# Dependences by bank in a wide PSUM buffer, and branch bits made one product later, in an attention and mixture-of-experts kernel

## Chip, cores and metric

One NeuronCore of a Trainium2 chip runs the whole program. The metric is the device time of one execution in microseconds (us), as the median of several. The engines are TensorE (PE, matrix products; PEld is its weight load, PEq and PEldq its sequencer), VectorE (DVE), ScalarE (ACT), GpSimd (POOL) and SyncE (SP, which issues most DMAs). Each engine works through its own instructions in order; semaphores hold one engine back for another.

## What is computed

An attention with queries averaged in pairs makes 2304 rows of 512, and these go through a mixture of 8 experts, of which each row uses its best two:

```python
q_pool = q.reshape(B, H, S // factor, factor, D).mean(axis=3)
scores = scale * np.matmul(q_pool, k.transpose(0, 1, 3, 2))
...
attn_out = np.matmul(attn, v)                    # 4 x 8 x 576 x 64 -> 2304 x 512
...
noisy_logits = logits + noise_scale * noise
top2 = np.argpartition(-noisy_logits, 2, axis=1)[:, :2]
...
for e in range(E):
    for k in range(2):
        mask = top2[:, k] == e
        h = np.maximum(x[mask] @ w1[e], 0.0)
        out[mask] += top2_w[mask, k, None] * (h @ w2[e])
```

Inputs and output are float32. Products of the experts are made of three fp16 products (high by high, high by low, low by high), so x, h and the weights each exist as a high and a low half.

## The kernel before

The attention and the routing are issued in an order that a planner (`Plan`) sets ahead of time from costs and due times. As soon as rows of a batch are routed, POOL scatters them, sorted by expert, to a buffer xg in DRAM, and DMA transposes bring them back as columns. The experts then run in `Moe`:

- `early` is still planned. It works on the first 256 rows (`EARLY`) of experts 0, 1 and 2 while the last batch is being routed. For each of the 8 slices f of the hidden layer, `one` calls `mm1`: 12 matmuls of 128x256 (L1067), four chunks of the inner dimension by three fp16 products. Then `act` makes hh, the high half of the relu, on ACT (L1131), and `low` makes hl, the rest, on DVE (L1135). For experts 0 and 1 the second layer follows (`mm2`, L1102, and `out_y`, L1107).
- `run` is in the order in which it is written. For expert 0 it takes rows 256 to 608 (`CUT`), so each main product is 12 matmuls of 128x352 out of xTg, and `flush` makes hh (ACT L1094) and hl (DVE L1095). After the eighth product `tail` holds rows 608 to 640 behind a branch: PE compares bit e of the register `s.more` and skips the block if the expert has no more rows than that. The bits come from four small DVE operations on the row counts (full, L1174 to L1178), and `values_load` (L1179) brings them into PE's register. Both stand before the first main product.

PSUM holds four single banks (psm) and two wide buffers of two banks each, `s.B.wides` (pss_63 and pss_64 in the program). A main product takes a wide buffer. An early product takes one half, that is one bank, from the pool "half": half 0 and half 1 of pss_63, half 0 and half 1 of pss_64, and again. The framework keeps track of dependences by the whole buffer: an instruction on one half that writes, or reads what was written, is ordered behind the last accesses of the other engines to either half.

The other names are: mk, a mask of the routing, which DVE makes (L870) for a small matmul (L873); mg, the gate factors that DVE makes in `meta` (L1050); wh and wl, the high and low halves of weights, split by ACT (L1016) and DVE (L1018); sp, a single element that POOL copies out of xTg (L1170) so that POOL waits for that transpose.

Of the kernel before, what the change touches and what calls it, by code (L numbers as in the profile page):

```python
# [9 lines left out]
F32 = mybir.dt.float32  # L10
I32 = mybir.dt.int32
U32 = mybir.dt.uint32
U16 = mybir.dt.uint16
AF = mybir.ActivationFunctionType
ALU = mybir.AluOpType
AX = mybir.AxisListType
# [3 lines left out]
P = 128  # L20
# [8 lines left out]
E = 8  # L29
# [3 lines left out]
CUT = 608  # L33
# [3 lines left out]
EARLY = 256  # L37
# [183 lines left out]
class Attn:  # L221
# [137 lines left out]
    def max_fin(s, i, c, g):  # L359
        V = s.nc.vector  # L360
        mx, qn2 = s.maxes(i), s.G.buf["qn2", i]
        m = s.rest(i, g)[:, SG:SG + c.stop - c.start]
        V.reduce_max(m, mx[:, c], axis=AX.X)
        V.tensor_scalar(qn2[:, c, 64], m, -1.0 / MC, None, op0=ALU.mult)
        V.scalar_tensor_tensor(qn2[:, c, 65], m, -1.0 / MC, qn2[:, c, 64], op0=ALU.mult, op1=ALU.subtract)

# [292 lines left out]
class Route:  # L659
# [111 lines left out]
    def steps(s, j, gs, tag, gap, L=None):  # L771
        nc = s.nc
        V = nc.vector
        C = 3 * len(gs)
# [26 lines left out]
        yield  # L801
        V.tensor_scalar(a, a, 87.0, None, op0=ALU.min)
        yield
# [134 lines left out]
class Moe:  # L938
# [115 lines left out]
    def mm1(s, e, f, a=0, b=CUT, ps=None):  # L1054
        nc = s.nc
        hi, lo = s.W[e, "1"]
        xT = s.X[e, a]
        hh, hl = s.H[e]
        if ps is None:
            ps = s.B.wide()  # L1060
        m = 1 if b - a <= 512 else 2
        N = (b - a) // m
        n = 0
        for dc in range(4):
            for w, x in ((hi, 0), (hi, 1), (lo, 0)):
                for i in range(m):
                    nc.tensor.matmul(ps[:, i, 0:N], w[:, dc, f * P:(f + 1) * P],  # L1067
                                     xT[:, 2 * dc + x, i * N:(i + 1) * N], start=(n == 0), stop=(n == 11))
                n += 1
        v = lambda t: t[:, f, a:b].rearrange("p (a n) -> p a n", a=m)  # L1070
        s.late.append((v(hh), v(hl), ps[:, 0:m, 0:N]))

    def tail(s, e, a):
        nc = s.nc
        n = CAP - CUT
        hi, lo = s.W[e, "1"]
        xT = s.X[e, a]
        hh, hl = s.H[e]
        ps = s.B.bank()[:, 0:8 * n].rearrange("p (f n) -> p f n", n=n)
        with s.tc.If((s.more & (1 << e)) > 0, preferred_fallthrough_block=False):  # L1080
            for f in range(8):
                k = 0
                for dc in range(4):
                    for w, x in ((hi, 0), (hi, 1), (lo, 0)):
                        nc.tensor.matmul(ps[:, f], w[:, dc, f * P:(f + 1) * P], xT[:, 2 * dc + x, CUT - a:CAP - a],
                                         start=(k == 0), stop=(k == 11))
                        k += 1
        s.late.append((hh[:, :, CUT:CAP], hl[:, :, CUT:CAP], ps))
        s.flush()
# [27 lines left out]
    def early(s, A):  # L1117
        G = A.G
        op = G.op
        nc = s.nc  # L1120
        A.M = s
        s.W[0, "1"] = s.F0.w
        for e in range(E):
            s.H[e] = s.H[e % 2] if e > 1 else tuple(s.h.tile([P, 8, CAP], F16, name=f"h{x}") for x in "hl")
        fl, ld, done = {}, {}, {}
        G.pool("half", [t[:, a] for t in s.B.wides for a in range(2)])
        last = None

        def act(e, f):
            hh, _, ps = fl[e, f]  # L1130
            nc.scalar.activation(hh, ps, AF.Relu)  # L1131

        def low(e, f):
            hh, hl, ps = fl[e, f]
            nc.vector.scalar_tensor_tensor(hl, ps, 0.0, hh, op0=ALU.max, op1=ALU.subtract)  # L1135

        def one(e, f):
            s.mm1(e, f, 0, EARLY, G.buf["m", e, f][:, None, :])
            fl[e, f] = s.late.pop()

        los = []
        A.xe[2] = op("SP", 1.4, LATE + 21, lambda: s.xload(2, 0, EARLY), lat=4.0)
        for x in range(16):
            e, nm, c = s.loads[x]
            key = LATE + (2, 13.512, 24.696, 36)[x // 4] + (2, 2.5, 2.5, 2.5)[x // 4] * c
            hi = op("ACT", 1.06, key, lambda e=e, nm=nm, c=c: s.split(e, nm, c, 0), deps=[ld[x]] if x in ld else ())
            los.append(op("DVE", 1.14, key, lambda e=e, nm=nm, c=c: s.split(e, nm, c, 1, False), deps=[hi]))
            for y in (4, 5, 6) if x == 0 else (x + 6,) if x < 4 else (x + 4,) if 5 < x < 12 else ():
                last = ld[y] = op("SP", 0.6, key, s.load, deps=los[x:x + 1] if y > 5 else (), lat=5.0, after=last)
            done.setdefault((e, nm), []).append(los[-1])  # L1150
        done[0, "1"] = [A.f0]
        for e in range(NFIRST):
            k0 = LATE + (-4.156, 23, 41.252)[e]
            mm, lows = None, []
            if e < NEARLY:
                mt = op("DVE", 0.8, k0 + 16, lambda e=e: s.meta(e, 0, EARLY), deps=[A.xe[e]])
            for f in range(8):
                mm = op("PE", 1.28, k0 + 1.3 * f, lambda e=e, f=f: one(e, f), deps=(done[e, "1"][f // 2:f // 2 + 1] if e else done[e, "1"]) + [A.xe[e]],
                        take=[("half", ("m", e, f))], after=mm)
                hi = op("ACT", 0.3, k0 + 1.3 * f + 1, lambda e=e, f=f: act(e, f), deps=[mm])  # L1160
                lows.append(op("DVE", 0.33, k0 + 1.3 * f + 1.5, lambda e=e, f=f: low(e, f), deps=[hi], give=[("m", e, f)]))
            for b in range(2 if e < NEARLY else 0):
                for q in range(4):
                    mm = op("PE", 1.28, k0 + 12 + 5 * b + 1.3 * q, lambda e=e, b=b, q=q: s.mm2(e, b, (2 * q, 2 * q + 1), G.buf["y", e, b]),
                            deps=lows[2 * q:2 * q + 2] + done[e, "2"][q:q + 1] if b == 0 else (), take=[("bank", ("y", e, b))] if q == 0 else (), after=mm)
                op("ACT", 0.55, k0 + 17 + 5 * b, lambda e=e, b=b: s.out_y(e, b, G.buf["y", e, b]), deps=[mm, mt], give=[("y", e, b)])
        G.run()

    def run(s):
        s.nc.gpsimd.tensor_copy(s.B.sp, s.X[0, EARLY][0:1, 7, CAP - EARLY - 1:CAP - EARLY])  # L1170
        s.put()
        V = s.nc.vector
        full = s.sm.tile([P, E + 1], F32, name="full", bufs=1)
        V.tensor_scalar(full[:, 0:E], s.R.n0, float(CUT), None, op0=ALU.is_gt)  # L1174
        V.tensor_mul(full[:, 0:E], full[:, 0:E], s.two)
        V.reduce_sum(full[:, E:E + 1], full[:, 0:E], axis=AX.X)
        mi = s.sm.tile([P, 1], I32, name="full_i", bufs=1)
        V.tensor_copy(mi, full[:, E:E + 1])  # L1178
        s.more = s.nc.values_load(mi[0:1, 0:1], engines=[mybir.EngineType.PE], min_val=0, max_val=(1 << E) - 1,  # L1179
                                  skip_runtime_bounds_check_because="it is only compared")  # L1180
        s.B.nw = 1
        for _ in range(4):
            s.load()
        for e in range(E + 1):
            if e == E:
                s.nc.gpsimd.drain()
            if e < E:
                if e == 2:
                    s.meta(e, 0, EARLY)
                s.meta(e, EARLY if e < NFIRST else 0, CAP)  # L1190
                for f in range(8):
                    s.mm1(e, f, EARLY if e < NFIRST else 0)
                    s.flush()
                    if 2 <= e < E - 1:
                        s.split(e + 1, "1", f // 2, f % 2)
                s.tail(e, EARLY if e < NFIRST else 0)
                if 1 <= e < E - 1:
                    s.xload(e + 1, EARLY if e + 1 < NFIRST else 0, CAP)
            if e:
                for k, b in enumerate(range(2 if e <= NEARLY else 0, NB)):  # L1200
                    if 2 <= e < E:
                        for c in ((k,), (k,), (2, 3))[k] if e == 2 else ((k,) if k < 4 else ()):
                            s.split(e, "2", c)
                    ps = s.B.bank()
                    s.mm2(e - 1, b, range(8), ps)
                    s.out_y(e - 1, b, ps)
# [142 lines left out]
```

## Time and profile before

| | |
|---|---|
| median of 3 runs | 849.32 us (849.32, 845.66, 850.34) |
| profiled execution | 846.78 us, its span 845.0 us |
| granted clock of PE over the span | 0.994 of full speed |
| busy share of PE, DVE, ACT, POOL | 93%, 60%, 53%, 49% |
| 412 to 476 us (early products) | PE busy 56.01 of 64 us |
| 476 to 508 us (expert 0, main products, tail) | PE busy 30.65 of 32 us |
| 508 to 836 us (the other experts) | PE busy 324.83 of 328 us |

A shown start and duration are those of one row of the trace. In square brackets at a row's end stands how long the engine was idle before it, and which instruction's semaphore released it. The end of a matmul is modelled: a row of x12 back to back lasts less than 12 single ones, since matmuls are pipelined.

### The profile page before, as it was taken

What the parts mean: (1) busy time and instruction counts of PE and PEld (TensorE: products, weight loads), DVE (VectorE), ACT (ScalarE), POOL (GpSimd) and SP (SyncE); (2) the same over time, 40 slices, a digit from 0 to 9 for tenths busy, and PEclk for the clock granted to TensorE, in tenths of its full rate; (3) what the DMA queues carried; (4) which work ended last, traced back from release to release, by engine and by line L of the source; (5) the groups of instructions that cost most, each with busy time, mean ns of one, the idle gap of its engine ahead of it and who ended that gap; (6) DMA issues with size and microseconds to landing.
All of it is one profiled execution on the core that took longest, in us unless ns stands there. A gap on an engine that the chain in (4) does not pass through costs nothing. (4 is left out here: it accounts for less than half of the span.)

```text
span 845.0 us, 21305 instructions
## 1 busy us (share of the span) xinstructions
PE 789.9 (93%) x8704; PEld 530.2 (63%) x8704; DVE 508.8 (60%) x1212; ACT 447.3 (53%) x702; POOL 417.2 (49%) x414
## 2 busy tenths in 40 slices
PE   4899899999999999999998899999999999999996
PEld 1666667777677776677855564565564755647442
DVE  5888898979898999999886231543152242422200
ACT  4778778888787777676644222433232332321310
POOL 4689887999789768777336302010202012020122
PEclk9999999999999999999999999999999999999999
DMA  8999988859998994889858902656628364381134
GB/s 202 205 220 214 223 198 204 202 164 211 208 212 187 180 231 103 197 180 264 204 168 284 253 13 31 180 153 140 161 76 225 76 180 95 105 209 13 26 41 61
DMA packets 214652, 137.32 MB, mean 163 GB/s; under 512 B 148240, under 2 KB 185616, under 8 KB 214544
## 3 DMA queue, kind: packets, MB, share of 16 engines
q1 hardware_dynamic: 205904, 115.74, 57.3%
q0 software_dynamic: 8640, 20.08, 11.9%
q8 instruction: 75, 1.23, 0.6%
q14 instruction: 33, 0.27, 0.1%
HBM read 62.14 MB, written 35.44 MB: 115 GB/s over the span
## 5 line engine op out<-in xcount | busy, mean ns | idle before, releaser
L394 POOL TENSOR_TENSOR pl<-pf 128x384 f16<-128x384 f32 x296 | 279.9, 977 | 54.8 <-ACT pf L386 42.1
L100 POOL DMA_INDIRECT out_dram<-y,mti x40 | 62.2, 1556 | 309.3 <-ACT y L1107 288.9
L386 ACT ACTIVATE pf<-pss 128x768 f32<-128x768 f32 x216 | 173.7, 815 | 54.4 <-PE pss L379 43.6
L414 PEld LDWEIGHTS <-pf 128*128 128x128 bf16 x2880 | 154.7, 98 | 47.1 <-issue 20.1
L414 PE MATMUL psm<-vv,pf 128*128 128x65 f16 (+1 forms) x2880 | 165.4, 194 | 5.9 <-DVE mx L338 3.0
L414 PE MATMUL psm<-vv,pl 128*128 128x65 f16 (+1 forms) x1440 | 157.1, 193 | 3.0 <-DVE pl L391 2.1
L378 PE MATMUL pss<-qt,kt 128*128 128x384 f16 (+1 forms) x576 | 147.8, 286 | 3.0 <-ACT pf L386 2.8
L379 PE MATMUL pss<-qt,kt 66*128 66x384 f16 (+1 forms) x576 | 148.3, 287 | 1.2 <-DMA qt<-qn 1.2
L1095 DVE SCALAR_TENSOR_TENSOR hl<-pss,hh 128x608 f16<-128x608 f32 (+1 forms) x64 | 44.3, 692 | 157.4 <-ACT hh L1094 157.0
L414 PEld LDWEIGHTS <-pl 128*128 128x128 f16 x1440 | 126.5, 99 | 5.3 <-issue 2.7
L1102 PE MATMUL psm<-wh,hh 128*128 128x512 f16 x320 | 121.3, 379 | 3.5 <-PEq L1080 3.5
L1102 PE MATMUL psm<-wh,hl 128*128 128x512 f16 x320 | 121.3, 379 | 0.0
L1102 PE MATMUL psm<-wl,hh 128*128 128x512 f16 x320 | 121.3, 379 | 0.0
L1102 PEld LDWEIGHTS <-hh 128*128 128x128 f16 x640 | 62.0, 98 | 78.4 <-issue 5.0
L338 DVE CUSTOM_DVE_ANT_0 rd<-psm,rd 128x512 f32<-128x512 f32 x144 | 97.6, 683 | 18.5 <-ACT rd L334 17.8
L1107 ACT ACTIVATE y<-psm,mg 128x512 f32<-128x512 f32 x40 | 27.5, 686 | 144.9 <-PE psm L1102 73.2
L1094 ACT ACTIVATE hh<-pss 128x608 f16<-128x608 f32 (+1 forms) x64 | 38.2, 597 | 114.1 <-PE pss L1067 114.1
L334 ACT ACTIVATE rd<-psm 128x512 f32<-128x512 f32 x144 | 85.8, 598 | 14.5 <-PE psm L318 12.5
L318 PE MATMUL psm<-kt,qt 128*128 128x128 f16 (+3 forms) x317 | 75.0, 308 | 8.8 <-DVE mx L338 4.1
L391 DVE TENSOR_TENSOR pl<-pf 128x768 f16<-128x768 f32 x68 | 74.5, 1115 | 2.3 <-ACT pf L386 2.3
L379 PEld LDWEIGHTS <-kt 66*128 66x128 f16 x576 | 56.1, 97 | 18.9 <-issue 4.7
L378 PEld LDWEIGHTS <-kt 128*128 128x128 f16 x576 | 56.2, 98 | 17.2 <-issue 4.0
(227 smaller groups left out, 1184.6 us busy)
## 6 DMA issues: line engine op xcount, KB each, us to landing
xg<-zt SPq DMA_DIRECT2D x40, 260.0 KB
kr<-in_k_dram SPq DMA_DIRECT2D x32, 288.0 KB
vr<-in_v_dram SPq DMA_DIRECT2D x16, 576.0 KB
kr<-in_moe_w_dram SPq DMA_DIRECT2D x16, 512.0 KB
qr<-in_moe_w_dram SPq DMA_DIRECT2D x16, 512.0 KB
kn<-in_moe_w_dram SPq DMA_DIRECT2D x16, 512.0 KB
qr<-in_q_dram SPq DMA_DIRECT2D x31, 256.0 KB
vr<-in_moe_w_dram SPq DMA_DIRECT2D x14, 512.0 KB
```

The lines of the kernel that those rows point to most:

```text
L100: i = nc.gpsimd.indirect_dma_start(out=out, out_offset=bass.IndirectOffsetOnAxis(ap=idx, axis=0), in_=src, in_offset=None, **kw)
L318: s.nc.tensor.matmul(ps[r, o:o + m.shape[1] * P], s.G.buf["qt", i][:, c, r], m, start=True, stop=True)
L334: s.nc.scalar.activation(s.G.buf["rd", i, c], s.G.buf["D", i, c], AF.Relu)
L338: s.nc.vector.tensor_tensor_reduce(out=rd, in0=s.G.buf["S", i, c], in1=rd, scale=1.0, scalar=-3.0e38, op0=ALU.add, op1=ALU.max, accum_out= ...
L378: mm(ps[:, a, o:o + w], kt[:, hh * NK + kc, :], qf[:, q0:q0 + w], start=True, stop=False)
L379: mm(ps[:, a, o:o + w], kt2[0:66, hh * NK + kc, :], qf2[0:66, q0:q0 + w], start=False, stop=True)
L386: s.nc.scalar.activation(s.parts(u)[0], s.G.buf["ps", u][:, :, 0:SG], AF.Exp, scale=0.125 / (IN_SCALE * IN_SCALE))
L391: s.nc.vector.tensor_sub(pl, pf, ph)
L394: s.nc.gpsimd.tensor_sub(pl[:, a], pf[:, a], ph[:, a])
L414: mm(o[:, 0:x], src[:, t % 2, ci * P:ci * P + P], vv[:, hh * NK + kc, a:a + x], start=st, stop=last and src is pl, skip_group_check=True)
L1095: s.nc.vector.scalar_tensor_tensor(hl, ps, 0.0, hh, op0=ALU.max, op1=ALU.subtract)
L1102: s.nc.tensor.matmul(ps, h[:, f, b * P:(b + 1) * P], w[:, f, :], start=(f == 0 and k == 0), stop=(f == 7 and k == 2))
```

## The change

Two things. First, `early` notes for each half which instructions touch it, and `apart` declares to the framework that an instruction on one half doesn't depend on an instruction of another engine on the other half of the same buffer ("distinct banks"). `mm1` returns its matmuls for this. Second, the four DVE operations become `counts`, which is called after the flush of the first main product, and the load of the register moves into `tail` of expert 0, ahead of its branch.

```diff
@@ mm1
+        made = []
...
-                    nc.tensor.matmul(ps[:, i, 0:N], w[:, dc, f * P:(f + 1) * P],
-                                     xT[:, 2 * dc + x, i * N:(i + 1) * N], start=(n == 0), stop=(n == 11))
+                    made.append(nc.tensor.matmul(ps[:, i, 0:N], w[:, dc, f * P:(f + 1) * P],
+                                                 xT[:, 2 * dc + x, i * N:(i + 1) * N], start=(n == 0), stop=(n == 11)))
...
+        return made
+
+    def counts(s):
+        V = s.nc.vector
+        full = s.sm.tile([P, E + 1], F32, name="full", bufs=1)
+        V.tensor_scalar(full[:, 0:E], s.R.n0, float(CUT), None, op0=ALU.is_gt)
+        V.tensor_mul(full[:, 0:E], full[:, 0:E], s.two)
+        V.reduce_sum(full[:, E:E + 1], full[:, 0:E], axis=AX.X)
+        s.full = s.sm.tile([P, 1], I32, name="full_i", bufs=1)
+        V.tensor_copy(s.full, full[:, E:E + 1])
@@ tail
         ps = s.B.bank()[:, 0:8 * n].rearrange("p (f n) -> p f n", n=n)
+        if e == 0:
+            s.more = nc.values_load(s.full[0:1, 0:1], engines=[mybir.EngineType.PE], min_val=0, max_val=(1 << E) - 1,
+                                    skip_runtime_bounds_check_because="it is only compared")
         with s.tc.If((s.more & (1 << e)) > 0, preferred_fallthrough_block=False):
@@ early
-        G.pool("half", [t[:, a] for t in s.B.wides for a in range(2)])
+        halves = [t[:, a] for t in s.B.wides for a in range(2)]
+        G.pool("half", halves)
+        used = [[] for _ in halves]
...
+        def apart(e, f, eng, made):
+            k = next(k for k, t in enumerate(halves) if t is G.buf["m", e, f])
+            for i in made:
+                for x, o in used[k ^ 1]:
+                    if x != eng:
+                        s.tc.declare_no_dep(i.ins, o.ins, reason="distinct banks")
+                used[k].append((eng, i))
...
-            nc.scalar.activation(hh, ps, AF.Relu)
+            apart(e, f, "ACT", [nc.scalar.activation(hh, ps, AF.Relu)])
...
-            nc.vector.scalar_tensor_tensor(hl, ps, 0.0, hh, op0=ALU.max, op1=ALU.subtract)
+            apart(e, f, "DVE", [nc.vector.scalar_tensor_tensor(hl, ps, 0.0, hh, op0=ALU.max, op1=ALU.subtract)])
...
-            s.mm1(e, f, 0, EARLY, G.buf["m", e, f][:, None, :])
+            apart(e, f, "PE", s.mm1(e, f, 0, EARLY, G.buf["m", e, f][:, None, :]))
@@ run
-        V = s.nc.vector
-        full = s.sm.tile([P, E + 1], F32, name="full", bufs=1)
...
-        s.more = s.nc.values_load(mi[0:1, 0:1], engines=[mybir.EngineType.PE], min_val=0, max_val=(1 << E) - 1,
-                                  skip_runtime_bounds_check_because="it is only compared")
...
                     s.flush()
+                    if e == f == 0:
+                        s.counts()
```

In the order of instructions, POOL and SP keep theirs. On ACT the rows keep their places and some conditions change. Here is ACT at the first products of expert 1, before the change (the line numbers 1107 and 1131 become 1121 and 1155 after it):

```order
L1107 ACTIVATE y<-psm_68,mg 128x512 [waits PE_49]
L1131 ACTIVATE hh<-pss_63 128x256 [waits PE_49]
L1131 ACTIVATE hh<-pss_63 128x256 [waits DVE_49]
L1131 ACTIVATE hh<-pss_64 128x256 [waits PE_49]
L1131 ACTIVATE hh<-pss_64 128x256 [waits DVE_49]
L1131 ACTIVATE hh<-pss_63 128x256 [waits PE_49]
L1016 ACTIVATE wh_8545<-qr 128x1024 [waits DMAHW5_49]
L1131 ACTIVATE hh<-pss_63 128x256 [waits DVE_49]
```

And ACT at the same place in the changed kernel:

```order
L1121 ACTIVATE y<-psm_68,mg 128x512 [waits PE_49]
L1155 ACTIVATE hh<-pss_63 128x256 [waits PE_49] x2
L1155 ACTIVATE hh<-pss_64 128x256 [waits PE_49] x2
L1155 ACTIVATE hh<-pss_63 128x256 [waits DVE_49,PE_49]
L1016 ACTIVATE wh_8545<-qr 128x1024 [waits DMAHW5_49]
L1155 ACTIVATE hh<-pss_63 128x256 [waits DVE_49,PE_49]
L1016 ACTIVATE wh_8545<-kn 128x1024 [waits DMAHW6_49]
```

The second relu of each pair waited for DVE; now it waits for PE (x2 stands for two rows that read alike).

DVE between the last early products and the first main ones, before:

```order
L1135 SCALAR_TENSOR_TENSOR hl<-pss_64,hh 128x256 [waits Activation_49] x2
L1174 TENSOR_SCALAR full<-n_8739 128x8
L1175 TENSOR_TENSOR full<-full,two 128x8 [waits DVE_49,Pool_49]
L1176 TENSOR_REDUCE full<-full 128x1 [waits DVE_49]
L1178 CAST full_i<-full 128x1 [waits DVE_49]
L1038 TENSOR_SCALAR mq<-mt 128x6 [waits DMAHW4_49]
```

and after (L1109 is what L1095 was, L1078 to L1082 what L1174 to L1178 were):

```order
L1050 TENSOR_SCALAR mg<-mg 128x3 [waits DVE_49]
L1109 SCALAR_TENSOR_TENSOR hl<-pss_63,hh 128x352 [waits Activation_49]
L1078 TENSOR_SCALAR full<-n_8739 128x8
L1079 TENSOR_TENSOR full<-full,two 128x8 [waits DVE_49,Pool_49]
L1080 TENSOR_REDUCE full<-full 128x1 [waits DVE_49]
L1082 CAST full_i<-full 128x1 [waits DVE_49]
L1109 SCALAR_TENSOR_TENSOR hl<-pss_64,hh 128x352 [waits Activation_49]
```

The four operations that make the bits went behind the gate factors (`meta`, ending in mg) and the subtraction of the first main product.

PE at the end of expert 0's main products in the changed kernel; before the change the TENSOR_LOAD stood, with the same list of semaphores, ahead of the first product that reads xTg:

```order
L1068 LDWEIGHTS fl
L1068 MATMUL pss_64<-xTg,fl 128x352
L1092 TENSOR_LOAD full_i [waits DMASW6_49,DMASW7_49,DMASW5_49,DMAHW0_49,DMASW4_49,DMAHW1_49,DMASW3_49,DMAHW2_49,DMASW2_49,DMAHW3_49,DMASW1_49,DMAHW4_49,DMASW0_49,DMAHW5_49,DVE_49,DMAHW6_49,PE_49,DMAHW7_49,Activation_49,Pool_49]
L1094 REGISTER_ALU
L1094 COMPARE_AND_BRANCH
L1094 UNCONDITIONAL_BRANCH [waits PE_49]
L1099 LDWEIGHTS fh
```

The load now stands behind the eighth main product and right ahead of the comparison that needs it.

## Rows read from the trace of the kernel before

**Rows 1.** The page: busy us and share of the span, instructions.

```profile
PE 789.9 (93%) x8704; PEld 530.2 (63%) x8704; DVE 508.8 (60%) x1212; ACT 447.3 (53%) x702; POOL 417.2 (49%) x414
```

**Rows 2.** Stretches: start:end, length, busy us (instructions) of PE, PEld, DVE, ACT, POOL; PEclk, DMA share, GB/s.

```profile
412.00:476.00 64.00, 56.01 (x437) 40.33 (x437) 43.05 (x169) 28.53 (x52) 25.03 (x31) 1.00 0.78 237
476.00:508.00 32.00, 30.65 (x192) 19.22 (x191) 9.19 (x28) 7.54 (x17) 3.12 (x2) 0.95 0.40 89
508.00:836.00 328.00, 324.83 (x1916) 186.96 (x1917) 95.51 (x158) 98.51 (x135) 54.37 (x35) 1.00 0.49 113
475.00:480.00 5.00, 3.56 (x15) 1.95 (x15) 1.27 (x12) 0.46 (x1) 0.00 (x0) 0.73 1.02 328
```

**Rows 3.** PE's waits from 412 to 508 us: total us, times, longest us.

```profile
PE pss L1067 <- DVE hl L1135: 3.9, 3, 1.9
PE pss L1067 <- DVE mg L1050: 3.4, 1, 3.4
PE psm L873 <- DVE mk L870: 1.1, 2, 0.8
PE pss L1067 <- PEq L1080: 0.6, 1, 0.6
```

**Rows 4.** PE in order of time: start us, us, instruction, [idle before <-releaser].

```profile
422.39 0.27 PE L1067 MATMUL pss<-xe,fl 128*128 128x256 f16 x1
423.02 0.38 PE L1067 MATMUL pss<-xe,fh 128*128 128x256 f16 x2 [0.36 <-DVE hl L1135]
...
444.72 0.38 PE L1067 MATMUL pss<-xe,wh 128*128 128x256 f16 x2 [1.59 <-DVE hl L1135]
...
461.15 1.47 PE L1067 MATMUL pss<-w1x 128*128 128x256 f16 x12 [1.95 <-DVE hl L1135]
...
476.44 0.46 PE L1067 MATMUL pss<-xTg,fh 128*128 128x352 f16 x2 [3.38 <-DVE mg L1050]
476.74 0.31 PE L1067 MATMUL pss<-xTg,fl 128*128 128x352 f16 x1
...
481.70 0.46 PE L1067 MATMUL pss<-xTg,fh 128*128 128x352 f16 x2
```

**Rows 5.** ACT in order of time, the first two relus of expert 1.

```profile
441.36 0.38 ACT L1131 ACTIVATE hh<-pss 128x256 f16<-128x256 f32 x1 [2.11 <-PE psm L875]
442.24 0.38 ACT L1131 ACTIVATE hh<-pss 128x256 f16<-128x256 f32 x1 [0.49 <-DVE hl L1135]
```

**Rows 6.** DVE in order of time.

```profile
426.26 0.42 DVE L1135 SCALAR_TENSOR_TENSOR hl<-pss,hh 128x256 f16<-128x256 f32 x1 [1.29 <-ACT hh L1131]
...
441.78 0.43 DVE L1135 SCALAR_TENSOR_TENSOR hl<-pss,hh 128x256 f16<-128x256 f32 x1 [0.44 <-ACT hh L1131]
...
474.80 0.16 DVE L1174 TENSOR_SCALAR full<-n 128x8 f32<-128x8 f32 x1
...
475.46 0.15 DVE L1178 CAST full_i<-full 128x1 int32<-128x1 f32 x1
...
479.90 0.53 DVE L1095 SCALAR_TENSOR_TENSOR hl<-pss,hh 128x352 f16<-128x352 f32 x1 [3.60 <-ACT hh L1094]
```

**Rows 7.** PE's sequencer by line: ns min/median/max, first to last start us.

```profile
L1179 PEldq EVENT_SEMAPHORE  x10: 51/51/3951, 471.0 to 475.8; - x10
L1179 PEldq TENSOR_LOAD <-full_i x1: 491/491/491, 475.9 to 475.9; - x1
...
L1080 PEldq ALU_OP  x8: 36/36/42, 490.2 to 782.2; - x8
L1080 PEldq EVENT_SEMAPHORE  x8: 51/51/51, 492.6 to 784.7; - x8
```

**Rows 8.** POOL in order of time: the twelve scatters' first and last, the copy sp.

```profile
443.99 1.19 POOL L100 DMA_INDIRECT xg<-xr,rta  x1 [3.14 <-ACT hh L1131]
...
459.89 1.72 POOL L100 DMA_INDIRECT xg<-xr,rta  x1 [0.30 <-issue]
...
468.34 0.18 POOL L1170 CAST sp<-xTg 1x1 f32<-1x1 f16 x1 [6.73 <-DMA xTg<-xg]
```

More of the change, by code (lines that the diff above doesn't have):

```diff
@@ L1171, in run @@
         s.put()
-        V = s.nc.vector
-        full = s.sm.tile([P, E + 1], F32, name="full", bufs=1)
[L1174 to L1178, printed above, removed]
-        s.more = s.nc.values_load(mi[0:1, 0:1], engines=[mybir.EngineType.PE], min_val=0, max_val=(1 << E) - 1,
-                                  skip_runtime_bounds_check_because="it is only compared")
         s.B.nw = 1
```

## Prediction, made before the changed kernel was run

> **What bounds the kernel now.** I read the page first, then busy time by stretch, then the waits of TensorE (PE) in the stretch that the diff touches, then that stretch in order of time. PE is busy 93% of the span [rows 1]. From 508 us on it has hardly a hole: 324.83 of 328 us at a granted clock of 1.00 [rows 2]. So whatever comes earlier there comes out at the end, one for one, as long as nothing else becomes late. From 412 to 476 us, where the early products run, PE is busy 56.01 of 64 us [rows 2]. The waits name what it waits for: 3.9 us in three waits for the DVE subtraction L1135, 1.1 us in two waits for the route's mask (mk, L870), 3.4 us in one wait put down to DVE mg [rows 3]. That last one is really the load of the branch bits: the ten semaphore waits of L1179 run from 471.0 to 475.8, one of them 3.951 us long, and the load, at 475.9 for 0.491 us, ends at 476.39, where the first main product starts at 476.44 [rows 4, 7]. The long one waits for the CAST full_i at 475.46 on DVE [rows 6], which stands behind the last early subtractions.
>
> **A stall costs more than its idle figure.** Twelve 128x256 matmuls in a row take 1.47 us and one is shown as 0.27, so starts lie (1.47 − 0.27)/11 = 0.11 apart [rows 4]. The shown idle begins at the modelled end, 0.16 after the next could have started. Each stall costs its figure and 0.16.
>
> **Part 1, the halves.** Before, ACT's relu of half 0 waits for PE's product into half 1, and its relu of half 1 waits for DVE's subtraction in half 0: the row at 442.24 was released by hl, 0.88 us after the relu before it began [rows 5]. PE's next product into half 0 waits for the subtraction of half 1. After, each waits for its own half alone, which is freed a product earlier. The order on each engine stays.
> - The three waits of PE on L1135 (0.36, 1.59, 1.95 [rows 4]): 3.90 + 3 × 0.16 = 4.38. I carried the trace's durations forward through the new waits, engine by engine, in program order: 0.17 is left for a subtraction of PE's own half behind a long weight split. So 4.21.
> - The two waits for mk: 1.13 together, the longer one 0.82 [rows 3], with 2 × 0.16 about 1.45. DVE makes mk behind subtractions which waited for ACT's late relus (1.29 idle at 426.26, 0.44 at 441.78 [rows 6]). With the relus earlier DVE comes to mk one to two us earlier, PE 0.5 to 0.9 earlier; the first wait goes and 0.12 of the second is left. So 1.33.
> - Two engines in the two banks of one buffer at once: no row shows this pair. The 128x256 relu and subtraction are shown at 0.38 and 0.42 while PE writes the other buffer [rows 5, 6]; I take the same. Were every one of the 24 relus and 24 subtractions twice as long, they would still be shorter than the 1.3 us that a product takes, so at most the part of the 4.21 us where DVE is packed, about 1 us, is at risk.
>
> **Part 2, the bits.** Four small DVE operations go from before the first main product to behind its subtraction; the load goes from before that product to the tail of expert 0.
> - Removed: 3.38 + 0.16 = 3.54 before the first main product. Its rows (xTg) are late next, see the rivals; the wide buffer it writes was left by early products two and more back.
> - The clock: in 475 to 480 us it was 0.73 [rows 2]. Full-speed starts of 128x352 matmuls lie 0.46 − 0.31 = 0.15 apart; the first two main products, 24 matmuls, took 481.70 − 476.44 = 5.26 [rows 4], against 24 × 0.149 = 3.58. So 1.68 was lost behind this wait, and none shows behind the shorter ones: 412 to 476 us ran at 1.00 [rows 2]. Without the wait the engine arrives at full clock: 1.68 gained.
> - The four DVE operations, 0.8 us from 474.80 to the end of CAST at 475.61 [rows 6], now fall into 3.60 us that DVE sat idle before the subtraction at 479.90 [rows 6]; a main product lasts 1.8, its subtraction 0.53. Cost 0. The subtraction queued behind them is late by at most 0.8 and PE needs its buffer a product later.
> - The load in the tail: from 471.0 to the last wait's end are 4.85 us, less the long one's 3.95 that is 0.9 for nine; with a tenth and the load's 0.49 it is 1.5 to 1.6 of PE's sequencer [rows 7]. That sequencer runs ahead of the array: in expert 0's tail its ALU_OP stands at 490.2, and then it waits until 492.6 for the array [rows 7], 2.4 us. The load's real condition, full_i, is over ten us old by then; its other semaphores are of the attention. So 1.6 hides in 2.4: cost 0. What stays is the 0.6 that the branch costs already [rows 3]. If the load does not run ahead, 0.5 to 1.7.
> - ACT's and PE's added semaphore conditions, POOL's and SP's order: nothing moves, 0.
>
> **Sum.** 4.21 + 1.33 + 3.54 = 9.08; the replay gives 9.04 at the first main product, which then starts at 467.4. With 1.68 for the clock, 10.7; at the most, with nothing left over, 4.38 + 1.45 + 3.54 + 1.68 = 11.05. The profiled execution took 846.78, so 836.1. It is 2.54 below the median of 849.32; on the median the forecast is **838.6**.
>
> **Rivals.**
> - *The transposed rows become the bound.* The first main product reads xTg, whose landing released POOL's sp cast at 468.34 [rows 8]. Twelve scatters from 443.99 to 459.89 [rows 8] come before the transpose. DVE starts them, and I have that about 2.07 earlier, so a landing near 466.2 against PE at 467.4: 1.2 us of room. If the scatters do not move, PE waits 0.9: 839.5. If faster weight loads crowd them and the landing comes at 470, PE waits 2.6, and with part of the clock's 1.68 given back the time is 841.2 to 842.9. For it: 461 to 476 us is where PE gains most and the DMA path least; DMA engines are busy 0.78 of 412 to 476 [rows 2]. Against: the order on POOL and SP is the same. The clock fell (0.73) after 3.38 us of idle and not (1.00) after 1.59 and 1.95 [rows 2, 4]. [...]
> - *The load isn't hidden in the tail* (it lets the array drain first). For it: before, no load stands behind unfinished matmuls, as PE was already idle. 1.6 on top: 840.2, and up to 841.9 if the clock falls.
> - *The declared independence brings nothing in the early stretch* (the change does not do what it says; or another semaphore holds the same instructions). Only 3.54 + 1.68 = 5.2 remains: 844.1. Against: in the order of ACT the waits of the second relu of a pair do change.
> - *Slower.* Weight loads issued up to 3.7 us earlier on SP meet the scatters and hold the xTg transpose up. Every us of its landing past 467.4 costs one, and the clock falls as now (1.68); the gain is used up when PE's first main product starts at 476.4 as before, that is by a landing at 476.4, 8.1 us later than now [rows 8]; from there each us is a loss, and a landing at 481 gives 849.3 + 4.6 = 853.9. Nothing in the rows points to so much.
>
> **How the numbers follow.** Forecast 0.62; transposed rows 0.17; load in the tail 0.11; no effect in the early stretch 0.08; slower 0.02. Low end: 11.05 off the lowest run shown, 845.66, is 834.6. High end 844.0: it takes in rivals one and two and nearly the third. A measurement of this kernel can tell about 0.5%, 4.2 us, from no change. Faster than 845.1 are the forecast, both next rivals and most of the third: 0.92; within 4.2 us the rest of the third: 0.06; slower 0.02.
>
> **What would show it.** In the profile of the changed kernel: no PE wait on L1135 of over 0.2 us from 412 to 476; no wait on mk of over 0.2; the first xTg matmul near 467.4 with idle under 0.2, and the clock 1.00 in the 5 us from it, the next 23 matmuls 0.15 apart; relus in pairs with no hl as releaser; the sp cast near 466.3, before the first xTg matmul; the wait at the branch of expert 0 still 0.6 with the load's end before the array's; from 500 us on everything 10.7 earlier. Wrong it would be by a wait on xTg above 1 us, by idle of 1 us or more at the tail of expert 0, or by a low clock behind the first main product.

## The result, and the profile after

The changed kernel takes 838.62 us (median of 6 runs, 833.73 to 841.84), the kernel before 847.73 (6 runs, 845.66 to 850.34). The ratio is 0.9881, 95% interval 0.9844 to 0.9918. A second measurement of the same kernel, beside the experiments, gave 0.9885 (0.9855 to 0.9915). The forecast was 838.6, that is a ratio of 0.9874 to the median of 849.32 known then, in a range of 834.6 to 844.0. That the two figures for the time agree to a tenth is luck, as single runs lie 8 us apart and the median of the kernel before came out 1.6 us lower with six runs: by the medians the gain is 9.1 us, in the two profiled executions 11.8, of which 10.87 lie behind the first early product. That the gain is some 10 us and where it comes from is not luck, as the profile shows.

The waits of PE from 412 to 498 us in the changed kernel (total us, times, longest us), to be held against [rows 3]:

```profile
PE pss L1068 <- PEq L1094: 0.6, 1, 0.6
PE psm L1116 <- PEq L1094: 0.4, 1, 0.4
```

The three waits on the subtraction, the two on mk and the long one in front of the first main product are gone. What is left belongs to the branches of the tails (the second line is expert 1's, which falls into this window now). The stretches, with the columns of [rows 2]:

```profile
412.00:466.00 54.00, 53.97 (x422) 39.22 (x419) 40.37 (x156) 28.37 (x51) 21.89 (x27) 1.00 0.70 231
466.00:498.00 32.00, 31.00 (x207) 19.85 (x205) 12.30 (x47) 8.34 (x19) 6.49 (x5) 1.00 0.78 151
498.00:824.00 326.00, 322.88 (x1908) 186.01 (x1906) 94.15 (x151) 98.03 (x133) 54.33 (x35) 1.00 0.49 113
466.00:471.00 5.00, 5.00 (x38) 3.45 (x36) 2.75 (x16) 1.31 (x3) 3.38 (x3) 1.00 1.14 204
```

PE is busy 53.97 of 54 us in the early stretch, where it was busy 56.01 of 64, and the clock is 1.00 in the 5 us that hold the start of the main products, where it was 0.73. The late stretch is what it was. PE and POOL around the first main product, the same instructions as in [rows 4, 8]:

```profile
466.61 0.46 PE L1068 MATMUL pss<-xTg,fh 128*128 128x352 f16 x2
466.91 0.31 PE L1068 MATMUL pss<-xTg,fl 128*128 128x352 f16 x1
...
470.19 0.46 PE L1068 MATMUL pss<-xTg,fh 128*128 128x352 f16 x2
```

```profile
441.01 1.18 POOL L100 DMA_INDIRECT xg<-xr,rta  x1 [2.60 <-DVE xr L901]
...
466.06 0.18 POOL L1194 CAST sp<-xTg 1x1 f32<-1x1 f16 x1 [6.89 <-DMA xTg<-xg]
```

There is no bracket ahead of the first xTg matmul: PE doesn't stop. The first two products take 470.19 − 466.61 = 3.58 us, where they took 5.26. The rows land just before they are needed, 466.06 against 466.61. And the load in the tail of expert 0, to be held against [rows 7]:

```profile
L1092 PEldq EVENT_SEMAPHORE  x10: 51/51/51, 478.7 to 479.7; - x10
L1092 PEldq TENSOR_LOAD <-full_i x1: 667/667/667, 479.8 to 479.8; - x1
...
L1094 PEldq ALU_OP  x8: 36/36/42, 480.5 to 770.7; - x8
L1094 PEldq EVENT_SEMAPHORE  x8: 51/51/51, 481.1 to 773.2; - x8
```

The ten waits and the load run from 478.7 to 480.5, ahead of the array, whose end the sequencer then awaits until 481.1. The stop there stays 0.6.

**How the runs are compared below.** The ten kernels of the experiments and the two of the result reach the first early product at times between 411.79 and 416.79 us, though none of them changes anything before it. So what comes after is measured from the start of that product's first row, in each one's profile. In us; "two products" are 24 matmuls:

| kernel | first early product at | to the first main product | two products | to the end of PE |
|---|---|---|---|---|
| before | 413.72 | 62.72 | 5.26 | 423.47 |
| changed | 413.13 | 53.48 | 3.58 | 412.60 |
| e1, changed again | 414.51 | 53.49 | 3.57 | 412.56 |
| e2, halves alone | 413.59 | 56.79 | 4.90 | 417.19 |
| e3, bits alone | 411.79 | 58.12 | 3.81 | 417.47 |
| e4, bits made early | 414.88 | 54.43 | 3.58 | 413.53 |
| e5, only products declared | 414.07 | 53.49 | 3.58 | 412.59 |
| e6, only relu and subtraction | 416.79 | 58.59 | 3.58 | 417.66 |
| e7, four loads | 413.71 | 53.48 | 3.58 | 414.27 |
| e8, rows late | 413.23 | 56.09 | 3.60 | 415.18 |
| e9, load further ahead | 412.90 | 53.49 | 3.58 | 412.65 |
| e10, one branch for two | 413.50 | 53.49 | 3.58 | 411.94 |

In the kernels without the old dependences the first main product comes after 53.48 or 53.49 us wherever PE has no stop ahead of it, and the four in which nothing costs PE time (changed, e1, e5, e9) end within 0.09 us of one another. So among these I take a difference of over 0.1 us as real, though each row is one profile. The three with the old dependences (before, e3, e6) differ by up to 1.07 us among themselves, and there only more than that counts. The ratios of whole runs are known to 1.6 us at best and 5 us at worst, to either side.

### The profile page after: what moved, and what is told of

It is laid out like the page before. It is cut to its first block, busy times and chain, and to the rows that moved or that the text cites. A ratio compares the mean times of both kernels' runs of the same rounds, so it can differ in the third digit from the quotient of the medians.

```text
span 833.2 us, 21316 instructions
## 1 busy us (share of the span) xinstructions
PE 785.7 (94%) x8704; PEld 528.4 (63%) x8704; DVE 510.0 (61%) x1212; ACT 447.7 (54%) x702; POOL 419.4 (50%) x414
## 5 line engine op out<-in xcount | busy, mean ns | idle before, releaser
L1109 DVE SCALAR_TENSOR_TENSOR hl<-pss,hh 128x608 f16<-128x608 f32 (+1 forms) x64 | 44.2, 691 | 153.0 <-ACT hh L1108 152.6
L391 DVE TENSOR_TENSOR pl<-pf 128x768 f16<-128x768 f32 x68 | 76.4, 1144 | 1.4 <-ACT pf L386 1.2
```

What stands on the lines that cost most here:

```text
L391: s.nc.vector.tensor_sub(pl, pf, ph)
L1109: s.nc.vector.scalar_tensor_tensor(hl, ps, 0.0, hh, op0=ALU.max, op1=ALU.subtract)
```

## The experiments

**e1, the changed kernel again.** No edit.

> The changed kernel unaltered, beside the ones that undo a part of it. All theories: 52.9 to 54.1 us from the first early product to the first main product (53.48 in its first profile), 3.6 us for the first two main products, ratio to the kernel before 0.985 to 0.991.

Measured: 836.03 us, 0.9885 (0.9855 to 0.9915), 53.49 and 3.57 us in the table. As expected.

**e2, the halves alone.** The bits go back in front of the first main product.

```diff
@@ run
         s.put()
+        s.counts()
+        s.more = s.nc.values_load(s.full[0:1, 0:1], engines=[mybir.EngineType.PE], ...
         s.B.nw = 1
...
-                    if e == f == 0:
-                        s.counts()
@@ tail
-        if e == 0:
-            s.more = nc.values_load(s.full[0:1, 0:1], engines=[mybir.EngineType.PE], ...
```

> The dependences by bank as in the changed kernel, but counts and load of the bits back in front of the first main product. My theory (sum of terms): the early stretch keeps its gain, and the load waits for a CAST behind the last early subtraction: subtraction ends 0.4 to 0.5 after the last relu, four operations 0.85, load 0.5 to 0.7, so the first main product comes about 2.6 us later than in the changed kernel, and shown idle is about 2.4. If the low clock belongs to any stop at this place, 1.7 more is lost in the first two main products (5.2 us for them, +4.3 in all, so 6.5 less than before); if a stop of this length does not bring it, 3.6 us for them, and +2.6 in all (8.2 less than before). Rival (the halves bring nothing, all comes from the bits): as before, +10.7.

Measured: 840.34 us, 0.9933 (0.9915 to 0.9952); 4.59 us more than the changed kernel by the end of PE, 6.28 less than before. The last early matmul starts 53.38 us after the first one, exactly as in the changed kernel, so the halves do all their work without the bits. Then PE stops. Its first rows, and the bits' rows on DVE and on PE's sequencer:

```profile
470.38 0.74 PE L1068 MATMUL pss<-xTg,fh 128*128 128x352 f16 x2 [3.13 <-DMA xTg<-xg]
470.92 0.50 PE L1068 MATMUL pss<-xTg,fl 128*128 128x352 f16 x1
```

```profile
467.69 0.42 DVE L1156 SCALAR_TENSOR_TENSOR hl<-pss,hh 128x256 f16<-128x256 f32 x1 [0.88 <-ACT hh L1152]
468.04 0.40 DVE L1078 TENSOR_SCALAR full<-n 128x8 f32<-128x8 f32 x1
...
468.93 0.15 DVE L1082 CAST full_i<-full 128x1 int32<-128x1 f32 x1
```

```profile
L1194 PEldq EVENT_SEMAPHORE  x10: 51/51/1733, 466.6 to 469.3; - x10
L1194 PEldq TENSOR_LOAD <-full_i x1: 952/952/952, 469.4 to 469.4; - x1
```

The bracket names the rows' DMA, but that landed by 466.6, where the first semaphore wait begins; the engine waited for the CAST, which ended at 469.08, and then for the load. The load took 0.952 us where it took 0.491 before, which is 0.46 of the 0.7 by which the stop of 3.13 exceeds the 2.4 that I expected. The clock fell again: matmuls of 352 columns shown at 0.50 in place of 0.31, 4.90 us for the two products, 1.32 lost.

**e3, the bits alone.** Dependences by the whole buffer, as before.

```diff
@@ apart
-                    if x != eng:
+                    if False:
```

> Counts and load as in the changed kernel, but dependences by the whole wide buffer as before. My theory: the waits on subtractions and mask come back (the trace of the changed kernel carried forward through the old waits gives 6.1 us more by the first main products, five waits on DVE in the early stretch), no stop in front of the first main product, full clock: 3.6 us for the first two. Time 6 more than the changed kernel, 4.7 less than before. Rival (the halves bring nothing): as the changed kernel, within 0.5. Rival (the stop moves elsewhere, to the tail of expert 0): idle there above 0.6.

Measured: 841.33 us, 0.9954 (0.9925 to 0.9983); 4.87 more than the changed kernel, 6.00 less than before, where I had expected 6 and 4.7. No stop in front of the first main product, and 3.58 us for two products but for a wait of some 0.2. The old waits are back in their places, though smaller:

```profile
PE pss L1068 <- DVE hl L1159: 2.8, 3, 1.4
PE psm L873 <- DVE mk L870: 1.1, 2, 0.8
PE pss L1068 <- PEq L1094: 0.6, 1, 0.6
```

The two longest on the subtraction, in order of time:

```profile
442.24 0.38 PE L1068 MATMUL pss<-xe,wh 128*128 128x256 f16 x2 [1.05 <-DVE hl L1159]
...
458.15 1.47 PE L1068 MATMUL pss<-w1x 128*128 128x256 f16 x12 [1.43 <-DVE hl L1159]
```

The three waits on the subtraction sum to 2.8 us where they were 3.9. One half of the difference is at the wait of 1.59 in [rows 4], now 1.05: before, the first relu of expert 1 began over 2 us late [rows 5, the row at 441.36]; here it follows the copy of y at once (437.46). That lateness was in the one profile of before and in neither of e3 and e6; what caused it stays open. The other half is at the wait of 1.95, now 1.43, behind weight splits that wait for a DMA. So the old dependences cost 4.6 to 5.7 us by the last early product, from one execution to the next: it starts 58.01 us after the first in e3, 58.48 in e6 and 59.08 before, against 53.38 without them.

**e4, the bits made early.** Counts on DVE behind the fourth early subtraction of expert 2, the load where it was before the change.

```diff
@@ low
+            if (e, f) == (2, 3):
+                s.counts()
@@ run
         s.put()
+        s.more = s.nc.values_load(s.full[0:1, 0:1], engines=[mybir.EngineType.PE], ...
...
-                    if e == f == 0:
-                        s.counts()
@@ tail
-        if e == 0:
-            s.more = nc.values_load(s.full[0:1, 0:1], engines=[mybir.EngineType.PE], ...
```

> As the changed kernel, but the counts are made on DVE behind the fourth early subtraction of expert 2, and the load stands in front of the first main product as it did before. It tells whether the place of the load costs anything, or only what it waits for. My theory: the CAST is done some 3 us before PE comes there, PE's sequencer runs about 2.4 us ahead of the array and needs 1.8 for the ten waits and the load: no idle, full clock, time as the changed kernel within 0.4. Rival (a load of a register stops the array where it stands, whatever it waits for): 0.7 to 1.8 us of idle in front of the first main product, +0.7 to 1.8.

Measured: 837.90 us, 0.9909 (0.9873 to 0.9945); 0.95 us more than the changed kernel in front of the first main product. My theory missed. The sequencer's rows, and POOL's copy that waits for the same rows:

```profile
L1195 PEldq EVENT_SEMAPHORE  x10: 51/51/51, 467.7 to 468.7; - x10
L1195 PEldq TENSOR_LOAD <-full_i x1: 488/488/488, 468.8 to 468.8; - x1
```

```profile
467.76 0.18 POOL L1193 CAST sp<-xTg 1x1 f32<-1x1 f16 x1 [6.72 <-DMA xTg<-xg]
```

None of the ten waits is long (51 ns at most), so nothing was still to come for the bits. But they begin at 467.7, when the rows land. In the order of PE the first main product's weight load, which waits for those rows, stands ahead of the load of the bits. The sequencer stands there until the rows land, loses its lead, and needs 1.6 us for waits and load afterwards. Without a stop PE would have gone on 53.48 us after the first early product, at 468.36, that is 0.66 after the rows landed; 1.6 less 0.66 leaves the 0.95 that was measured. That is a reading; e9 tries it.

**e5 and e6, which declaration it is.** Independence declared only between products and the other engines, or only between relu and subtraction.

```diff
@@ apart, e5
-                    if x != eng:
+                    if x != eng and "PE" in (x, eng):
@@ apart, e6
-                    if x != eng:
+                    if x != eng and "PE" not in (x, eng):
```

> As the changed kernel, but independence is declared only between products (PE) and the other two engines; between relu (ACT) and subtraction (DVE) of the two halves the order stays, so the second relu of a pair still waits for the first one's subtraction. It tells which declaration carries the gain. My carrying forward of the trace: 0.0 to 0.3 us more than the changed kernel by the first main product, no wait of PE above 0.3, since the subtraction of the first half ends before the second product does. Rival (my first reading, that relu and subtraction alternating is what makes PE wait): 2 us or more of the 5.5 come back.

> The reverse: independence declared only between relu and subtraction; products stay ordered against both halves. Carrying forward the trace: 5.9 us more than the changed kernel by the first main product, with the waits on DVE of the kernel before (0.5, 0.5, 1.0, 1.2, 2.9). Rival (relu and subtraction alternating is the cause): at most 3.5 us more.

Measured: e5 836.60 us, 0.9870 (0.9817 to 0.9922), and in the table the changed kernel to 0.01 us. e6 840.57 us, 0.9932 (0.9895 to 0.9969), 5.1 us more than the changed kernel by the first main product, with the old waits:

```profile
PE pss L1068 <- DVE hl L1159: 3.3, 3, 1.9
PE psm L873 <- DVE mk L870: 1.1, 2, 0.8
PE pss L1068 <- PEq L1094: 0.6, 1, 0.6
```

In e5 the relus still wait for the subtraction of the other half:

```profile
440.27 0.66 ACT L1155 ACTIVATE hh<-pss 128x256 f16<-128x256 f32 x2 [2.24 <-DVE hl L1159]
443.05 0.66 ACT L1155 ACTIVATE hh<-pss 128x256 f16<-128x256 f32 x2 [2.13 <-DVE hl L1159]
```

They come late and in pairs, and PE doesn't care: in e5 it has no wait on DVE at all. So the declarations that touch a product carry the whole gain, those between relu and subtraction none of it. Whether it is those between product and relu or those between product and subtraction, no run separates.

**e7, four loads in the tail.**

```diff
@@ tail
         if e == 0:
-            s.more = nc.values_load(s.full[0:1, 0:1], ...
+            s.mores = [nc.values_load(s.full[0:1, 0:1], ...) for _ in range(4)]
-        with s.tc.If((s.more & (1 << e)) > 0, preferred_fallthrough_block=False):
+        with s.tc.If((s.mores[e % 4] & (1 << e)) > 0, preferred_fallthrough_block=False):
```

> As the changed kernel, with four loads of the same bits into four registers in the tail of expert 0 in the place of one. The first has ten waits and took 1.8 us in all; each further one is 0.5 to 0.7 us. The sequencer is 2.4 us ahead, 0.6 of it left over. My theory (cover by running ahead): 1.8 + 3 x 0.67 = 3.8 against 2.4, so the stop in the tail grows from 0.6 by 1.2 to 1.5. Rival (a load does not hold the array at all): 0.6 as it is. Rival (loads run one upon another): under 0.3 more.

Measured: 837.74 us, 0.9871 (0.9812 to 0.9930); the stop in the tail of expert 0 is 2.24 us, 1.68 more than 0.56, all of it still there at the end of PE (414.27 against 412.60).

```profile
483.91 0.47 PE L1068 MATMUL pss<-xTg,wh 128*128 128x352 f16 x2 [2.24 <-PEq L1094]
```

```profile
L1092 PEldq EVENT_SEMAPHORE  x10: 51/51/51, 479.3 to 480.2; - x10
L1092 PEldq TENSOR_LOAD <-full_i x4: 488/496/900, 480.3 to 482.1; - x4
...
L1094 PEldq ALU_OP  x8: 36/36/42, 483.1 to 773.0; - x8
L1094 PEldq EVENT_SEMAPHORE  x8: 51/51/51, 483.4 to 775.5; - x8
```

The chain runs from 479.3 to 483.1, 3.8 us; the array ended at 483.91 − 2.24 = 481.67, 2.4 us after the chain began. So 2.4 us of it hide in that lead and 1.4 stick out. The stop grew by a little more than the 1.2 to 1.5 that I expected, because the comparison behind the load, some 0.25 us from its ALU_OP to the wait that follows (483.1 to 483.4), doesn't hide any longer either.

**e8, the rows late.** The transposes of experts 0 and 1 change places on SP.

```diff
-                s.xl = [op("SP", 1.4, 430 + e, lambda e=e: s.M.xload(e, EARLY, CAP), ...) for e in range(NEARLY)]
+                s.xl = [op("SP", 1.4, 431 - e, lambda e=e: s.M.xload(e, EARLY, CAP), ...) for e in (1, 0)]
```

> As the changed kernel, but SP issues the transpose of expert 1's rows ahead of that of expert 0's, so that the rows of the first main product land as the second pair did (470 to 471.6 in the changed kernel's time, against 466.0). It prices the rival of the late rows. My theory: PE stops 3.5 to 5.0 us in front of the first main product, and the clock falls as it did behind 3.4 us of idle, 1.7 more in the first two main products: +5.2 to +6.7 in all. Rival (the clock's fall belonged to the load of the bits, not to the idle time): +3.5 to 5.0, first two main products 3.6 us. Rival (the rows are not what PE waits for): 0.

Measured: 838.04 us, 0.9895 (0.9839 to 0.9951); 2.6 us more than the changed kernel.

```profile
469.32 0.47 PE L1068 MATMUL pss<-xTg,fh 128*128 128x352 f16 x2 [2.44 <-DMA xTg<-xg]
469.63 0.31 PE L1068 MATMUL pss<-xTg,fl 128*128 128x352 f16 x1
```

```profile
469.00:474.00 5.00, 4.67 (x32) 3.09 (x33) 2.58 (x14) 0.93 (x2) 3.38 (x3) 1.00 0.93 315
```

PE does wait for the rows, 2.44 us, and starts at 469.32: the rows land sooner than the 470 to 471.6 that I expected, so the loss is below what the theory (5.2 to 6.7) and the first rival (3.5 to 5.0) gave. And behind this stop the clock stays at 1.00, 3.60 us for two products. So in this execution the rows cost their lateness and no more. Whether a later landing would also cost the clock, e8 doesn't show. Nor does it show that the clock's fall belongs to the load of the bits: the last section has falls without any load.

**e9, the load further ahead.** As e4, with the load ahead of the last early product.

```diff
@@ one
+            if (e, f) == (2, 7):
+                s.more = nc.values_load(s.full[0:1, 0:1], engines=[mybir.EngineType.PE], ...
```

> As e4 (counts made on DVE behind the fourth early subtraction of expert 2), but the load stands ahead of the last early product of expert 2, not behind the weight load of the first main product, which waits for the transposed rows. e4 stopped PE for 1.05 us, and its first semaphore wait of the bits began at 467.74, when the rows landed (467.7). It tells whether a load anywhere ahead of a product stops the array, or only one that stands behind that wait. My theory now (the sequencer's lead is lost at the wait for the rows): no stop at the load and none in front of the first main product, 53.4 to 53.6 us from the first early product to the first main one, time as the changed kernel. Rival (only the tail can hide a load): 0.7 to 1.1 us more.

Measured: 836.80 us, 0.9860 (0.9804 to 0.9917), 53.49 us to the first main product. No stop at the load or behind it:

```profile
L1162 PEldq EVENT_SEMAPHORE  x10: 51/51/51, 463.1 to 464.1; - x10
L1162 PEldq TENSOR_LOAD <-full_i x1: 490/490/490, 464.2 to 464.2; - x1
```

Waits and load end at 464.7, while the array works on to the first main product at 466.39. So the reading of e4 holds: the load costs nothing where the sequencer has its lead, and behind a wait it costs what sticks out over the work that the array has left.

**e10, one branch for two.** What is left in the profile of the changed kernel is the stop at each of the eight branches. Experts 0 and 1 share one here.

```diff
@@ run
-                s.tail(e, EARLY if e < NFIRST else 0)
+                if e != 0:
+                    s.tail((e - 1, e) if e == 1 else (e,))
@@ tail
...
-        with s.tc.If((s.more & (1 << e)) > 0, preferred_fallthrough_block=False):
+        with s.tc.If((s.more & sum(1 << e for e in es)) > 0, preferred_fallthrough_block=False):
+            for i, e in enumerate(es):
...
```

> As the changed kernel, but the tails of experts 0 and 1 share one branch, behind the main products of expert 1, with the load ahead of it. The stop at a branch that isn't taken is 0.56 shown idle, 0.72 with the 0.16 behind the last matmul, seven more times later on. My theory: one stop less, 0.7 us less from the first early product to the end of PE than in the changed kernel (411.9 against 412.6), not to be told from it by the times. Rival (the stop belongs to the change of operands, not to the branch): the same 412.6. Rival (the later tail holds up the second layer of expert 0): a new wait of PE psm on ACT or DVE, 0.3 or more.

Measured: 838.05 us, 0.9863 (0.9821 to 0.9906); 411.94 us from the first early product to the end of PE, 0.66 less than the changed kernel. The waits of PE from 466 us on, of e10:

```profile
PE psm L1119 <- PEq L1091: 3.1, 6, 0.6
PE psm L1119 <- ACT hh L1111: 0.6, 1, 0.6
```

One of the eight stops is gone, and one of the others is put down to ACT at the same length, as one is in e9, where no branch was joined. By one profile this version beats both kernels, by 0.66 us over the changed one; the times can't tell it from that.

## Why the prediction was right

Step by step, with 10.7 us forecast and 423.47 − 412.60 = 10.87 measured:

- *The halves and mk, 4.21 + 1.33 = 5.54.* The last early matmul starts 59.08 us after the first one before and 53.37 after: 5.71. The 0.17 and 0.12 that I left standing didn't show. The term was read from one profile, and e3 and e6 show that this profile was at its upper end: another would have given 4.6 or 5.1, and a whole gain of 9.8 or 10.3. That the term fits to 0.2 is in part luck.
- *The stop at the load, 3.54.* From the last early matmul to the first main one it was 3.64 and is 0.11: 3.53.
- *The clock, 1.68.* 5.26 − 3.58 = 1.68. e2 brings 1.32 of it back with a stop of 3.13.
- *The load in the tail, 0.* The stop is 0.56 as before. The cover was thinner than I had it: waits and load took 1.77 and not 1.5 to 1.6, out of the 2.4 that e7 shows. e7 also shows that the cover was needed.
- *DVE's four operations, 0.* They sit at 469.5 to 470.4, behind the first main product's subtraction, and PE has no wait on DVE.
- *Two engines in the two banks of one buffer, at risk for about 1 us.* The risk didn't come true: in the changed kernel the relus of the early products last 0.36 to 0.39 us and the subtractions 0.41 to 0.43, as before, while PE writes the other half.

What was not right, without a consequence for the time:

- *The mechanism of part 1.* I named three orders: relu behind the other half's product, relu behind the other half's subtraction, and product behind it. The second costs nothing (e5, e6); the other two together carry the gain, and no run tells them apart. The 0.88 us between two relus, which I read out of [rows 5] as a sign of the cause, was beside the point. A wait of an engine that is not the bound proves nothing until the bound engine waits for it.
- *The room ahead of the rows.* I had 1.2 us; it is 466.61 − 466.06 = 0.55. The start of the scatters came forward as forecast (2.98 by the clock of the trace, 2.4 counted from the first early product), but PE gained a little more than I gave it, and some scatters were slower. The rival was half a microsecond away, and nearer in e1, where the copy sp starts at 467.73 and the first main product at 468.00; in e10 it is 465.06 against 466.99.
- *The price of that rival.* For a wait of 2.6 I gave 841.2 without and 842.9 with the clock's fall on top. e8 has a wait of 2.44 and no fall, which is the lower of the two. The Trainium skill, "TensorE: Matmul & The Clock Gate", section "HAM oscillation — how this bites in real kernels", has the next group of matmuls start cold behind a DMA wait that is long enough. No run here shows a fall behind a DMA wait: the 3.13 and 3.38 us of idle, behind which the clock did fall, were spent on the load of the bits.
- *What bits and halves bring apart.* 6.28 for the halves alone and 6.00 for the bits alone make more than 10.87. By the table the halves alone give 5.70 in the early stretch, and of the stop and the low clock they already give 0.23 and 0.36, as the CAST came 6.4 us earlier. The bits alone come out 1.07 better only because the old waits were shorter in that execution. Without the doubly counted 0.59 and the 1.07 it is 10.6; e3's wait between the first two main products is the remaining 0.2.
- *The chances.* I counted 0.02 of the third rival's 0.08 as faster than 845.1 and called it most of it; as its 844.1 lies below 845.1, the 0.92 should have been above 0.94.

That declared independence brings nothing is excluded by e2, e3 and e6, and that the load can't hide by the profile after with e7 and e9.

## What to carry to other kernels

A dependence that the framework tracks for a whole buffer is worth undoing where it holds the bound engine; declare those orders first, and look in the trace whether the others cost anything. A register load for a branch cost nothing here where what it reads was old, no instruction ahead of it on the same engine waited, and its waits and load together (1.77 us) fitted into the sequencer's lead (2.4 us): place it behind long work and not right behind the wait for a transfer. Measure from a point that all versions share: here the runs scatter by 5 us before the change even begins, and the stretch behind repeats to 0.05 us from the changed kernel to its repetition, e1. Where waits remain it can still vary, by 1 us under the old dependences.

## What the runs showed of the hardware that was not expected

- PE's clock behind a stop in front of the first main product: none lost after 2.44 us of idle (e8), 1.32 us after 3.13 (e2), 1.68 after 3.38 (before). These are one execution each and give no limit in idle time: early in the attention, where PE waits for ACT and loads no register, the clock went to half of full speed at 43.8 us behind a stop of 1.97 us (before) and at 43.0 behind one of 1.85 (e2), and it stayed at full speed behind one of 2.10 that ended at 43.3 (changed kernel). The fall isn't tied to the moment at which PE goes on either: in front of the first main product the clock fell 0.8 us after PE had resumed in the kernel before (477.3 against 476.44), and 0.7 us ahead of that in e2 (469.7 against 470.38). The stretch with the low level in e2:

```profile
470.00:475.00 5.00, 4.62 (x23) 2.62 (x23) 0.52 (x1) 0.46 (x1) 0.87 (x1) 0.69 1.01 288
```

- The load of the bits' register on PE took 0.483 (e5) to 0.952 us (e2) in these profiles. The ten semaphore waits ahead of it start 0.11 apart even where every semaphore was set, 1.1 us in all in the changed kernel (478.7 to 479.8), more than its load of 0.667.
- The sequencer's lead over the array was 2.4 us at the end of expert 0's main products (e7). Behind an unmet wait, there a weight load's, it was down to the 0.66 us of work that the array had left when the wait was met (e4).
